# Pooling v for three attention pairs: two additions per pair on VectorE, with a fourth buffer for the pooled loads

## Chip, cores and metric

One Trainium2 chip, one core. The metric is the device time of the kernel in microseconds (us); lower is better. The engines are named as in the profile: PE (TensorE), DVE (VectorE), ACT (ScalarE), POOL (GpSimd), SP (SyncE); PEld is TensorE's loading of weights.

## The reference

Attention on q, k, v of shape 8 x 8 x 576 x 64 (batch, heads, sequence, head width), once on sequences pooled 4:1 by a mean, once in a band of three positions to either side; the two are added, and the sum goes through a gated feed-forward layer (512 to 1536 to 512):

```python
q_d, k_d, v_d = [t.reshape(B, H, Sd, 4, D).mean(axis=3) for t in (q, k, v)]
out_up = np.repeat(sm_attn(q_d, k_d, v_d), 4, axis=2)
mask = np.abs(pos[:, None] - pos[None, :]) < 4
out_local = softmax(where(mask, scale * q @ k.T, -1e9)) @ v
x = (out_up + out_local).transpose(0, 2, 1, 3).reshape(B * S, H * D)
out = (np.maximum(x @ w_gate, 0) * (x @ w_val)) @ w_out
```

## The kernel before

Two heads of one batch entry form a *pair*; there are 32 pairs, numbered `hp` in order of work. Each pair goes through: loads of q, k and v (`emit_in`), the transposed q and k (`emit_qkT`, a transposing DMA from SP's queue for pairs from 9 on), their 4:1 sums (`emit_pool`, L309, one DVE reduction), the scores (`emit_s1_mm`, L389 and L400), the exponentials on ACT (L410, L424), the masking on DVE (`emit_mask`, L416), the products with v (`emit_s2w_mm`, L552 and L560), the division (L570, L575 on ACT, L579 on DVE) and the sum of both attentions into `xT` (`emit_xsum`, L538). After four pairs a 512-token chunk of the feed-forward layer can run: `emit_h_mm` (L622) multiplies by the two weights, L639 (ACT) and L643 (DVE) form the gated product, L652 or, in the later part, the seven products of L719 with sums on DVE (L713) multiply by the last weight.

*Pooled v.* For pairs below 9 it is made by TensorE (`emit_vd`). From pair 9 on, v is loaded a second time by `emit_load_v4` (L297) so that the four positions to be summed lie in one partition (72 partitions of 4 x 256). Two additions follow: `emit_v2` (L355) adds the two halves of each 256, float16 in and float32 out, 512 elements a partition; `emit_v1` (L361) adds the two halves of that, 256 elements a partition, float16 out, into `vd`. Both run on POOL. `v4` is a ring of 3 buffers (`NV4`), `v2` one of 2, `vd` one of 3. `vd` of a pair is read by the matmuls of L560.

*Order.* Every engine's instructions are in an order written out by hand, and each engine takes its own in that order; waits between engines follow from the tiles. The first four pairs are a fill; then come slots `s` = 0 to 7 (`emit_slot`), slot `s` working on pair `hp = s + 4` and loading pair `hp + 4`; then the periods of four pairs (`ORDER`), then a tail. In a slot, `emit_slot_in` comes first. It puts on POOL: the four half loads of q and k of pair `hp + 4`, then the additions of pair `hp + 1` (v2, v1), then the load of v and the v4 load of pair `hp + 4`. So pairs 9, 10 and 11 are pooled in slots 4, 5 and 6; in slot 6 v2 of pair 12 follows at once, and slot 7 does v1 of pair 12 and v2 of pair 13. POOL's queue carries these loads as well as its own arithmetic; SP's carries the transposes and most of the output.

On DVE, slot 5 begins after the weight difference L685 at the end of slot 4, with `emit_pool` of pair 9, then a gate (L643). Slot 6 begins after xsum of pair 9 with the masks of pair 10; slot 7 after xsum of pair 10 with the masks of pair 11. In the periods, `after/3/0` (L1019) is a copy on POOL that makes it wait until the DVE sums of an earlier unit are there and TensorE has read the old ones.

`q32` holds q of the first pair as float32 (L257) until ACT converts it; it isn't used again until the sums of the tail. `zero_sb` feeds warm-up matmuls with zeros.

Of the kernel before, what the change touches and what calls it, by code (L numbers as in the profile page):

```python
# [10 lines left out]
FP16 = mybir.dt.float16  # L11
AF = mybir.ActivationFunctionType
ALU = mybir.AluOpType
# [89 lines left out]
def _dap(t_ap: bass.AP, extra_off: int, dims) -> bass.AP:  # L103
    return bass.AP(tensor=t_ap.tensor, offset=t_ap.offset + extra_off, ap=list(dims))
# [13 lines left out]
def kernel(  # L118
# [10 lines left out]
    nc = tc.nc  # L129
# [13 lines left out]
    LEAD = 4  # L143
    NTP = 9
    NVP = 9
    VS = 7
    NK = NJJ // 2
    B0 = 1
# [4 lines left out]
    keep = ctx.enter_context(tc.tile_pool(name="keep", bufs=1))  # L153
# [2 lines left out]
    ffn = ctx.enter_context(tc.tile_pool(name="ffn", bufs=3))  # L156
    ypool = ctx.enter_context(tc.tile_pool(name="ypool", bufs=4))

    zero_sb = keep.tile([128, 640], FP16, name="zero_sb")
    cst_sb = keep.tile([128, 1368], FP16, name="cst_sb")  # L160
    masks_sb = cst_sb[:, 0:576]
    pool_sb = cst_sb[:, 576:960].rearrange("p (s c) -> p s c", s=3)
# [7 lines left out]
    def ring(n, shape, dtype, name):  # L170
        return [keep.tile(shape, dtype, name=f"{name}{i}") for i in range(n)]

    NL = 7
    NV4 = 3
    PS = 8
    qkfull = ring(NL, [128, 2, 2 * NB * 64], FP16, "qk16_")
    qk16 = [t[0:96] for t in qkfull]
    v4 = ring(NV4, [72, 4, 256], FP16, "v4_")
    v2full = ring(2, [128, 4, 128], FP32, "v2_")
    v2 = [t[0:72] for t in v2full]  # L180
# [6 lines left out]
    vd = ring(3, [72, 2, 192], FP16, "vd_")  # L187
# [6 lines left out]
    q32full = keep.tile([128, 2 * NB * 64], FP32, name="q32")  # L194
# [3 lines left out]
    ps = psum.tile([128, 8, 512], FP32, name="ps")  # L198
# [41 lines left out]
    def head_off(hp):  # L240
        b = (hp // NPB + B0) % B
        return b, (b * H + 2 * (hp % NPB)) * S * D
# [51 lines left out]
    def emit_load_v4(hp):  # L294
        b, off = head_off(hp)
        if hp >= NVP:
            nc.gpsimd.dma_start(  # L297
                v4[hp % NV4], _dap(v, off, [[4 * D, 72], [72 * 4 * D, 4], [1, 4 * D]])
            )

    def emit_qkT(hp):
        nc.sync.dma_start_transpose(
            out=qkT[hp % 4][:, 0 : 2 * S].rearrange("p (n t) -> p n t", t=NQ),
            in_=qk16[hp % NL].rearrange("p i c -> p (i c)"),
        )
# [10 lines left out]
    def emit_qkT_pe(hp, b0, b1, b0_last=False):  # L316
        r, r4, r2 = hp % NL, hp % 4, hp % 2
        sv = qk16[r].rearrange("p i (h j d) -> p i h j d", h=2, d=64)
        blocks = list(range(2 * NB))
        if hp == 0:  # L320
            blocks = blocks[NB:] + blocks[:NB]
        elif b0_last:
            blocks = blocks[4:] + blocks[:4]
        for n in blocks:
            lo = 120 * (n % 4)
            bank = b0 if n < 4 else b1 + n // 4 - 1
            for hh in range(2):
                nc.tensor.matmul(  # L328
                    out=ps[64 * hh : 64 * hh + 64, bank, lo : lo + 120],
                    lhsT=sv[:, n // NB, hh, n % NB, :],  # L330
                    rhs=eyesum_sb,
                    start=True,
                    stop=True,
                )
        big = qkT[r4][:, 0 : 2 * S].rearrange("p (b n t) -> p b n t", b=3, n=4)
        sml = qkd[r2].rearrange("p i t -> p (i t)").rearrange("p (b n t) -> p b n t", b=3, n=4)
        act, dve = nc.scalar.copy, nc.vector.tensor_copy
        if hp == 0:
            plan = ((2, 1, act), (2, 0, act), (1, 1, dve), (1, 0, dve), (0, 1, act), (0, 0, dve))
        elif b0_last:  # L340
            plan = ((1, 1, act), (1, 0, act), (2, 1, dve), (2, 0, dve), (0, 1, dve), (0, 0, act))
        else:
            plan = ((0, 1, act), (0, 0, act), (1, 1, dve), (2, 1, dve), (2, 0, dve), (1, 0, act))
        for i, pooled, copy in plan:
            bank = b0 if i == 0 else b1 + i - 1
            t = ps[:, bank, 0:480].rearrange("p (n t) -> p n t", n=4)
            if pooled:
                copy(out=sml[:, i], in_=t[:, :, 96:120])
            else:
                copy(out=big[:, i], in_=t[:, :, 0:96])  # L350

    def emit_v2(hp):
        if NVP <= hp < NP:
            t, m = v4[hp % NV4], v2[hp % 2]
            nc.gpsimd.tensor_tensor(out=m, in0=t[:, :, 0:128], in1=t[:, :, 128:256], op=ALU.add)  # L355

    def emit_v1(hp):
        if not NVP <= hp < NP:
            return
        m, o = v2[hp % 2], vd[hp % 3]  # L360
        nc.gpsimd.tensor_tensor(  # L361
            out=o.rearrange("p c (x d) -> p x c d", x=3)[:, 0:3:2, :, :],
            in0=m[:, :, 0:64].rearrange("p (h c) d -> p h c d", h=2),
            in1=m[:, :, 64:128].rearrange("p (h c) d -> p h c d", h=2),
            op=ALU.add,
        )
# [64 lines left out]
    def emit_s1(hp, p0):  # L431
        emit_s1_mm(hp, p0)
        for g in range(2):
            emit_exp(hp, p0, g)
            emit_mask(hp, g)
        emit_ed(hp, p0)
# [182 lines left out]
    def emit_h_mm(c, jj, pp, which, kks, out=None):  # L619
        w = (wg_sb, wv_sb)[which]  # L620
        for kk in kks:
            nc.tensor.matmul(  # L622
                out=pair(pp)[:, which, :] if out is None else out,
                lhsT=w[:, kk, bass.ts(jj, 128)],
                rhs=xT[:, kk, c * TCH : (c + 1) * TCH],
                start=(kk == 0),
                stop=(kk == 3),
            )
# [179 lines left out]
    def emit_in(hp, between=lambda: None):  # L808
        if hp >= NP:
            between()  # L810
            return
        if 4 <= hp < NL:
            nc.gpsimd.memset(vw[hp][:, :, 64:128], 1.0)
        emit_load_qk(hp)
        between()
        emit_load_v(hp)
        emit_load_v4(hp)
        if hp in after_load:
            emit_wslice(after_load[hp])
        if hp == 8:  # L820
            for i in range(4):
                emit_wo(i)

    def emit_warm(n):
        for _ in range(n):
            nc.tensor.matmul(
                out=ps[:, 7, :], lhsT=zero_sb[:, 0:128], rhs=zero_sb[:, 128:640], start=True, stop=True
            )

    def emit_fill(hp):  # L830
# [240 lines left out]
    def emit_slot_in(s):  # L1071
        hp = s + LEAD
        if s < VS:
            def pools():
                emit_v2(hp + 1)
                emit_v1(hp + 1)
                if s == VS - 1:
                    emit_v2(hp + 2)
            emit_in(hp + 4, pools)
        else:  # L1080
            emit_v1(hp + 1)
            emit_in(hp + 4, lambda: emit_v2(hp + 2))
        if NTP <= hp + 3 < NP:
            emit_qkT(hp + 3)

    def emit_slot(s, gate):
        c, jj, hp = s // 4, 3 * (s % 4), s + LEAD
        emit_slot_in(s)
        if s == 0:
            emit_qkT_pe(hp, 2, 3)  # L1090
            emit_h_mm(c, jj, 3, 1, range(3))
            emit_h_mm(c, jj, 3, 0, range(1))
            emit_x_pe(hp - 1, 0)
            emit_h(c, jj, 3, ((0, range(1, 4)), (1, range(3, 4))))()
            emit_s1(hp, 2)
            emit_h(c, jj + 1, 0)()
            emit_vd(hp, 6)
            emit_qkT_pe(hp + 1, 2, 3)
            return emit_h(c, jj + 2, 3)
        if s <= 5:  # L1100
            if s == 5:
                emit_pool(hp)
            else:
                gate()
                if s < 4:
                    emit_vd(hp, 1)
            emit_s2t(hp - 1, gate if s == 5 else lambda: None)
            if s == 4:
                emit_wt(0)
        elif gate:  # L1110
            gate()
        if s > 4:
            emit_y(c - 1, s % 4, 1 if s == 5 else 2, 6 if s == 5 else 2, lambda: emit_s1(hp, 4))
            emit_pool(hp + 1)
            if s == PS - 1:
                for step in LEAD_IN.split():
                    kind, arg = step.split("/")
                    emit_step(kind, arg, 1, c)
                return None
            emit_h(c, jj, 0)()  # L1120
            emit_wt(s - 3)
            emit_s2w(hp)
            emit_h(c, jj + 1, 1)()
            emit_h(c, jj + 2, 0)()
            emit_xsum(hp)
            return None
        if s == 4:
            emit_y(c - 1, s % 4, 1)
        else:
            emit_h(c, jj, 0)()  # L1130
        emit_s1(hp, 4)
        if s == 4:
            emit_h(c, jj, 0)()
        emit_h(c, jj + 1, 1)()
        if s == 4:
            emit_wt(1)
            emit_vd(hp, 5)
        else:
            emit_qkT_pe(hp + 1, 4, 0, True)
        return emit_h(c, jj + 2, 3)  # L1140
# [54 lines left out]
```

## Time and profile before

| what | value |
|---|---|
| time, median of 5 runs | 347.5 us (346.84 to 348.41) |
| the profiled execution | 347.17 us, span 345.3 us |
| POOL L355 (v2), 23 times | 1246 ns each |
| POOL L361 (v1), 23 times | 832 ns each |
| POOL L297 (v4 load), 23 times | 739 ns to issue, 6.4 us to landing |
| additions of pair 9 | v2 at 69.04, v1 at 70.28 us |
| additions of pair 10 | v2 at 76.09, v1 at 77.33 us |
| additions of pair 11 | v2 at 82.59, v1 at 83.83 us |

The profile is of one execution. "Busy" is the time in which an engine executed; the bracket behind a timeline line is the time for which its engine stood idle before it, and what it then got. An instruction's duration can hold time in which it is held up by another engine. The share of PE says how little of the span is left for any other engine to show in the time.

### The profile page before, as it was taken

The numbers are of one execution on the slowest core, as the hardware profiler recorded it, in microseconds if no ns is written. First come the engines' busy times: TensorE is split into PE (matmuls) and PEld (weight loads), VectorE is DVE, ScalarE is ACT, GpSimd is POOL, SyncE is SP. The second block draws the span as 40 slices with busy tenths as digits, with TensorE's granted clock in tenths as the row PEclk, the third lists the DMA queues.
The fourth block names the chain that finished last, engine by engine and source line by source line (L and its number), as shares of the span: only waits on it lengthen the run. The fifth ranks groups of instructions, "written<-read, shape, count | busy, mean of one in ns | idle before, by whom it ended". The sixth has DMA issues, their size and how long they took to land.

```text
span 345.3 us, 8168 instructions
## 1 busy us (share of the span) xinstructions
PE 336.4 (97%) x3187; PEld 210.8 (61%) x3187; DVE 294.1 (85%) x529; ACT 215.2 (62%) x410; POOL 189.7 (55%) x238
## 2 busy tenths in 40 slices
PE   6999999999999999999999999999999999999996
PEld 2665555555475656565666656665766557767685
DVE  5895567799899999999999999999999798786892
ACT  3767776677676676677667766776677634344222
POOL 8976556899999993969397797940300000000000
PEclk9999999999999999999999999999999999999999
DMA  9999999999999999999989996992000001001023
GB/s 144 164 171 185 187 189 168 164 171 183 162 153 179 159 180 86 121 148 176 106 102 138 170 124 79 170 125 64 31 32 31 32 0 47 30 33 53 32 69 109
DMA packets 168774, 40.31 MB, mean 117 GB/s; under 512 B 150080, under 2 KB 165664, under 8 KB 168736
## 3 DMA queue, kind: packets, MB, share of 16 engines
q0 software_dynamic: 132960, 22.93, 92.3%
q1 hardware_dynamic: 35056, 15.79, 24.5%
q10 hardware_dynamic: 720, 1.08, 0.9%
q8 instruction: 25, 0.41, 0.6%
q14 instruction: 13, 0.11, 0.1%
HBM read 46.45 MB, written 9.44 MB: 162 GB/s over the span
## 4 chain that ended last, share of the span: by engine, by line
PE 83%; DVE 10%; ACT 2%; DMA 2%; issue 2%; ACTq 0%; POOLq 0%
PE ps L622 44%; PE ps L719 18%; PE ps L929 4%; PE ps L552 3%; PE ps L652 2%; PE ps L389 2%; PE ps L328 2%; PE ps L400 2%; DVE xn L579 2%; DVE gT L643 2%; DVE ee L416 2%; DMA qk<-in_k_dram 2%; PE ps L560 1%; DVE xo L713 1%; ACT rden L570 1%
## 5 line engine op out<-in xcount | busy, mean ns | idle before, releaser
L622 PE MATMUL ps<-xT,wv_sb 128*128 128x512 f16 x432 | 109.3, 379 | 0.0
L622 PE MATMUL ps<-xT,wg_sb 128*128 128x512 f16 x352 | 89.1, 380 | 0.1
L643 DVE TENSOR_TENSOR gT<-r,ps 128x512 f16<-128x512 f16 x88 | 59.1, 680 | 11.9 <-ACT r L639 6.3
L639 ACT ACTIVATE r<-ps 128x512 f16<-128x512 f32 x88 | 52.3, 594 | 26.9 <-PE ps L622 26.7
L622 PEld LDWEIGHTS <-wv_sb 128*128 128x128 f16 x432 | 41.0, 98 | 41.7 <-issue 0.2
L622 PEld LDWEIGHTS <-wg_sb 128*128 128x128 f16 x352 | 32.0, 98 | 32.3 <-DVE xT L615 0.6
L579 DVE TENSOR_TENSOR xn<-ps,rden 64x720 f16<-64x720 f32 x46 | 41.6, 905 | 4.2 <-ACT rden L575 2.9
L570 ACT ACTIVATE rden<-ps 64x720 f32<-64x720 f32 x46 | 35.2, 765 | 15.7 <-PE ps L560 14.7
L410 ACT ACTIVATE ee<-ps 112x576 f16<-112x576 f32 x64 | 38.1, 647 | 10.8 <-PE ps L400 9.8
L267 POOL DMA_DIRECT2D qk<-in_q_dram x46 | 33.9, 742 | 6.7 <-DMA wo_sb<-in_moe_w_out_dram 2.8
L267 POOL DMA_DIRECT2D qk<-in_k_dram x46 | 33.8, 740 | 3.8 <-DMA v<-in_v_dram 2.8
L416 DVE TENSOR_TENSOR ee<-ee,cst_sb 112x576 f16<-112x576 f16 x64 | 33.0, 539 | 2.8 <-ACT ee L410 2.2
L292 POOL DMA_DIRECT2D vw<-in_v_dram x30 | 28.7, 958 | 8.8 <-PE ps L560 2.9
L719 PEld LDWEIGHTS <-gT 128*128 128x128 f16 x288 | 28.2, 98 | 8.6
L309 DVE TENSOR_REDUCE qkd<-qkT 128x288 f16<-128x1152 f16 x23 | 30.9, 1343 | 0.3 <-DMA qkT<-qk 0.3
L355 POOL TENSOR_TENSOR v<-v 72x512 f32<-72x512 f16 x23 | 28.7, 1246 | 1.9 <-DMA v<-in_v_dram 1.4
L719 PEld LDWEIGHTS <-xo 128*128 128x128 f16 x240 | 22.7, 97 | 6.1 <-DVE xo L713 0.3
L753 ACT COPY q<-ps 128x256 f32<-128x256 f32 x39 | 14.5, 371 | 18.5 <-PE ps L719 18.2
L719 PE MATMUL ps<-wo_sb,gT 128*128 128x256 f16 x192 | 24.9, 273 | 0.0
L538 DVE TENSOR_TENSOR xT<-xn 128x576 f16<-128x576 f16 x28 | 24.0, 857 | 0.6
L939 ACT COPY vw<-ps 128x256 f32<-128x256 f32 x30 | 10.8, 373 | 20.7 <-PE ps L929 13.8
L552 PE MATMUL ps<-ee,vw 112*128 112x96 f16 x276 | 20.5, 205 | 1.0 <-DVE ee L416 1.0
(116 smaller groups left out, 571.4 us busy)
## 6 DMA issues: line engine op xcount, KB each, us to landing
out_dram<-y_sb SPq DMA_DIRECT2D x20, 256.0 KB, 3.6
vw<-in_v_dram POOLq DMA_DIRECT2D x30, 168.0 KB, 6.3
qk<-in_q_dram POOLq DMA_DIRECT2D x46, 72.0 KB, 6.0
qk<-in_k_dram POOLq DMA_DIRECT2D x46, 72.0 KB, 6.1
v<-in_v_dram POOLq DMA_DIRECT2D x23, 144.0 KB, 6.4
out_dram<-y_sb SPq DMA_DIRECT2D x22, 128.0 KB, 1.7
wg_sb<-in_moe_w_gate_dram POOLq DMA_DIRECT2D x4, 384.0 KB, 10.0
wv_sb<-in_moe_w_val_dram POOLq DMA_DIRECT2D x4, 384.0 KB, 10.8
```

The source lines that it names most:

```text
L267: nc.gpsimd.dma_start(dst.rearrange("p (j h d) -> p j h d", h=2, d=64)[:, :, hh, :], _dap(src, off + hh * S * D, [[D, 96], [NQ * D, NB], [ ...
L292: nc.gpsimd.dma_start(t, _dap(v, base, [[D, WK], [NQ * D, n], [1, D]]))
L309: nc.vector.tensor_reduce(out=qkd[hp % 2].rearrange("p i t -> p (i t)"), in_=qkT[hp % 4][:, 0 : 2 * S].rearrange("p (t f) -> p t f", f=4), ...
L410: nc.scalar.activation(out=o, in_=ps[0:WK, p0 + 2 * g : p0 + 2 * g + 2, 0:288], func=AF.Exp, scale=scale)
L416: nc.vector.tensor_tensor(out=o, in0=o, in1=_sap(masks_sb, (0, WK), 288 * g, [[0, 2], [1, 288]]), op=ALU.mult,)
L552: nc.tensor.matmul(out=ps[:, bank, NQ * j : NQ * j + NQ], lhsT=vflat[:, v0 : v0 + 128], rhs=e[:, hh, lo : lo + NQ], start=True, stop=True,)
L570: nc.scalar.activation(out=rden[lo : lo + 64], in_=ps[de : de + 64, 4 + 2 * hh : 6 + 2 * hh, 0:360], func=AF.Ln)
L579: nc.vector.tensor_tensor(out=xn[lo : lo + 64], in0=ps[lo : lo + 64, 4 + 2 * hh : 6 + 2 * hh, 0:360], in1=rden[lo : lo + 64], op=ALU.mult,)
L622: nc.tensor.matmul(out=pair(pp)[:, which, :] if out is None else out, lhsT=w[:, kk, bass.ts(jj, 128)], rhs=xT[:, kk, c * TCH : (c + 1) * TCH],
L639: nc.scalar.activation(out=r1, in_=pair(pp)[:, 0, :] if h1 is None else h1, func=AF.Relu)
L643: nc.vector.tensor_tensor(out=gT[c % 2][:, jj, :], in0=r1, in1=pair(pp)[:, 1, :] if h2 is None else h2, op=ALU.mult)
L719: nc.tensor.matmul(out=out, lhsT=left[:, i, :], rhs=right[i], start=(first and i == 0), stop=(i == NK - 1), skip_group_check=True,)
```

## The change

For pairs below `VVP` = 12, that is 9 to 11, both additions are issued on DVE, and at the head of the slot of the pair itself (5 to 7) rather than on POOL one slot earlier. The float32 result of v2 goes to `q32`'s memory. `v4` gets a fourth buffer, and `zero_sb` loses 128 columns: the warm-up matmuls read the same zeros for both operands. Pairs from 12 on stay on POOL in their old places.

```diff
+    VVP = 12
-    zero_sb = keep.tile([128, 640], FP16, name="zero_sb")
+    zero_sb = keep.tile([128, 512], FP16, name="zero_sb")
-    NV4 = 3
+    NV4 = 4
...
+    def pooling(hp):
+
+        if hp < VVP:
+            return nc.vector, q32full[0:72, 0:512].rearrange("p (a b) -> p a b", a=4)
+        return nc.gpsimd, v2[hp % 2]
+
     def emit_v2(hp):
         if NVP <= hp < NP:
-            t, m = v4[hp % NV4], v2[hp % 2]
-            nc.gpsimd.tensor_tensor(out=m, in0=t[:, :, 0:128], in1=t[:, :, 128:256], op=ALU.add)
+            t, (eng, m) = v4[hp % NV4], pooling(hp)
+            eng.tensor_tensor(out=m, in0=t[:, :, 0:128], in1=t[:, :, 128:256], op=ALU.add)
 
     def emit_v1(hp):
         if not NVP <= hp < NP:
             return
-        m, o = v2[hp % 2], vd[hp % 3]
-        nc.gpsimd.tensor_tensor(
+        (eng, m), o = pooling(hp), vd[hp % 3]
+        eng.tensor_tensor(
...
-                out=ps[:, 7, :], lhsT=zero_sb[:, 0:128], rhs=zero_sb[:, 128:640], start=True, stop=True
+                out=ps[:, 7, :], lhsT=zero_sb[:, 0:128], rhs=zero_sb, start=True, stop=True
...
             def pools():
-                emit_v2(hp + 1)
-                emit_v1(hp + 1)
                 if s == VS - 1:
                     emit_v2(hp + 2)
             emit_in(hp + 4, pools)
...
         c, jj, hp = s // 4, 3 * (s % 4), s + LEAD
+        if hp < VVP:
+            emit_v2(hp)
+            emit_v1(hp)
         emit_slot_in(s)
```

## The prediction

> **What bounds the kernel now.** I read the page first (busy shares, then the chain that ended last), then TensorE's timeline between 55 and 132 us for the places where it stands still, then VectorE's and GpSimd's timelines of the same stretch, because the change moves work between these two.
>
> ```profile
> PE 336.4 (97%) x3187; PEld 210.8 (61%) x3187; DVE 294.1 (85%) x529; ACT 215.2 (62%) x410; POOL 189.7 (55%) x238
> PE 83%; DVE 10%; ACT 2%; DMA 2%; issue 2%; ACTq 0%; POOLq 0%
> ```
>
> TensorE is busy for 336.4 of 345.3 us, so anything done on another engine counts only where TensorE waits for it. The slots concerned are 5 (TensorE from 66.68 us), 6 (76.88) and 7 (86.04 to 95.82); their TensorE timeline has one wait, and the next one comes in the first period of the steady loop:
>
> ```profile
> 90.92 0.29 PE L552 MATMUL ps<-ee,vw 112*128 112x96 f16 x3 [0.46 <-DVE ee L416]
> 115.22 0.25 PE L389 MATMUL ps<-qkd 64*72 64x144 f16 x2 [0.33 <-DVE xn L579]
> ```
>
> Measured from start to start the first costs 0.62 us (the pair of L560 before it starts at 90.23 and needs 0.07) and the second 0.50 us (L719 starts at 114.07 and needs 0.65). Together 1.12 us: the most that the change can win near its place. The stages, with columns length, then PE, PEld, DVE, ACT, POOL busy:
>
> ```profile
> 82.00:90.00 8.00, 8.00 (x68) 4.06 (x65) 7.63 (x9) 5.70 (x9) 7.89 (x9) 1.00 1.79 156
> 90.00:97.00 7.00, 6.54 (x64) 3.71 (x61) 6.00 (x8) 4.36 (x9) 6.99 (x9) 1.00 2.11 179
> 97.00:105.00 8.00, 8.00 (x79) 5.83 (x72) 7.87 (x14) 6.04 (x12) 7.98 (x11) 1.00 2.12 156
> 105.00:115.00 10.00, 9.89 (x85) 5.74 (x83) 9.92 (x14) 6.67 (x12) 9.61 (x14) 1.00 1.80 188
> ```
>
> VectorE has 1.0 us idle in 90 to 97, and only 0.2 from 97 to 115: there a delay of VectorE is passed on. GpSimd is full all through. Then VectorE's and GpSimd's lines that decide:
>
> ```profile
> 65.39 0.95 DVE L685 TENSOR_TENSOR wt<-wo_sb,xT 128x1536 f16<-128x1536 f16 x1
> 66.26 1.34 DVE L309 TENSOR_REDUCE qkd<-qkT 128x288 f16<-128x1152 f16 x1
> 68.58 0.69 DVE L643 TENSOR_TENSOR gT<-r,ps 128x512 f16<-128x512 f16 x1 [0.98 <-ACT r L639]
> ...
> 82.59 1.16 POOL L355 TENSOR_TENSOR v<-v 72x512 f32<-72x512 f16 x1
> 82.67 1.90 DVE L685 TENSOR_TENSOR wt<-wo_sb,wt 128x1536 f16<-128x1536 f16 x1
> ...
> 87.94 1.27 POOL L361 TENSOR_TENSOR vd<-v 72x256 f16<-72x256 f32 x1
> 88.56 2.31 DVE L416 TENSOR_TENSOR ee<-ee,cst_sb 112x576 f16<-112x576 f16 x2
> 89.46 1.40 DVE L416 TENSOR_TENSOR ee<-ee,cst_sb 112x576 f16<-112x576 f16 x1
> ...
> 137.11 0.19 POOL L1019 COPY seen<-xo 128x1 f16<-128x1 f16 x1 [5.69 <-PE ps L719]
> ```
>
> The L685 beside a GpSimd addition takes 1.90 us, the one at 65.39 takes 0.95. The two masks of pair 11 take 2.31 us where those of pair 10 (79.39) take 0.82: this is what TensorE waits for at 90.92. And at 137.11 GpSimd has waited 5.69 us for TensorE, so a head start of GpSimd ends there.
>
> **What the Trainium skill says.** "SBUF — State Buffer", section "Who interferes with whom": a VectorE instruction with both inputs in SBUF and a GpSimd instruction that reads SBUF exclude each other, the later one waits for the whole of the earlier. The trace agrees: L685 at 82.67 has its own 0.95 us left from the end of L355 (83.75), and L361 behind it (83.83) takes 1.33 instead of 0.72. The section also says that `tensor_tensor` does not hold up descriptor generation. The trace is not so clean: the mask at 89.46 takes 0.95 us more than its usual 0.45 while GpSimd only issues DMAs. "VectorE: DVE Perf Modes", section "The perf-mode tier table": `tensor_tensor` gains its double rate only for 16-bit tensors; v2 writes float32, v1 reads it, so both go at the single rate. The same page, section on the errata, prices such an addition at (N+151)/0.96 ns: 691 ns for 512 elements, 424 for 256. The trace agrees for L538 (576 elements: 757 by the formula, 0.75 to 0.76 us shown).
>
> **The change part by part.** *Removed from GpSimd*: v2 and v1 of pairs 9, 10, 11: 1.16+1.28, 1.17+0.72, 1.16+1.33 = 6.8 us in slots 4, 5, 6. TensorE waits for no GpSimd work there, so this is worth nothing by itself. Everything queued behind goes earlier: per slot four qk loads, the v load, the v4 load, later v1(12), v2(13). Adding up GpSimd's own durations it reaches the v4 load of pair 15 at about 87 us instead of 94.16. The new wait is here: that load's buffer (15 mod 4) is pair 11's, which VectorE reads at about 88.6 to 89.3; behind it stand the loads of pairs 16 and 17; the first is needed for the transpose issued with scores(13), near 106, so nobody waits for them. The DMA queue may not take the issues that fast (GpSimd waited for it at 66.27 and 67.50), which only shrinks the head start. At L1019, about 105, it now has to wait for the sums of L713 that end at 102.05: some 3 us of lead are left, and none at 137.
>
> *Added to VectorE*: per slot v2 then v1, at the head of slots 5, 6, 7. v1 reads v2's output, so it starts after v2's end: 0.69+0.03+0.36 (v1's 0.42 less the 0.06 by which starts overlap in this trace) = 1.08 us from v2's start to the next instruction. Three times 1.08 = 3.2 us. Not in the trace of before: bounds are 0.42+0.28 if the double rate held (L904 and L713 of 512 and 256 elements) and 1.08+0.95 if one is held up as the mask at 89.46 was; I take 1.08.
>
> *Slot 5*: after L685. L309 goes from 66.26 to 67.34 and ends at 68.68; TensorE starts scores(9) at 68.97. The gate (L643) sat idle for 0.98 and goes from 68.58 to 68.62. Hidden, with 0.29 us to spare; past that scores(9) are late. The masks at 70.89, which lost 0.5 to v1(9) on GpSimd, get it back; no one waited.
>
> *Slot 6*: after xsum (L538, 78.72). The masks of pair 10 end at 81.3 instead of 80.2; TensorE needs the second at 82.0. If v2(12), now about 78.2 on GpSimd, holds xsum up by 0.6, they end at 81.9: just in time. Behind: L685 keeps its 0.95, so it ends near where it did (84.57), before L579 at 84.81. Hidden.
>
> *Slot 7*: L579 at 84.81 waits for ScalarE's inv as before, so the chain to xsum (87.89) stands. v2(11) starts at 88.56, v1 ends at 89.70, the masks run 89.64 to 90.46 if GpSimd holds nothing: v1(12), which cost them time at 87.94, has gone to about 81, and GpSimd waits for v2(11). TensorE goes on at 90.51 instead of 90.92: **0.4 us won**. L309(12) starts at 90.4 instead of 90.78; no lag is carried past the 0.5 and 0.4 us idle at 92.64 and 93.73.
>
> *First period*: GpSimd's additions meet other VectorE instructions. Before, four of these lost 0.42 (L713 at 99.35), 0.53 (100.97), 0.60 (L538, 106.35) and 0.84 us (L713, 111.91). About as many will meet; zero, with a bound of the 0.50 at 115.22 won to one v2 (1.16) lost.
>
> *Fourth v4 buffer*: v4 loads waited 0.3 us four times for v2 on GpSimd; off the path. *zero_sb by 128 columns*: about 0.13 us less memset; the first real matmul waits for k to land (6.56). Zero.
>
> Sum: -0.4 us. The profiled execution took 347.17, so 346.8; the median of the runs shown is 0.33 above it, so **347.1**.
>
> **Rivals.** A, *both waits go*: slot 7 is clean and the period's collisions thin out, -1.1 us: 346.4. For it: 2.4 us of VectorE's time there was lost to collisions. Against: GpSimd has the same six additions to do in that stage, only 3 us earlier.
> B, *the slot 7 masks end later than before* (the other side): four two-input instructions stand where two stood, GpSimd issues v4(15) and qk loads beside them, and two are held up by 0.95 as at 89.46. Masks end at 92.36, TensorE goes on 1.5 us later: 349.0. It decides once hold-ups in slot 7 exceed 0.41 us (2.31 less 1.08 less 0.82). For: the full VectorE behind. Against: the mask at 79.76, beside the same kind of issue, took 0.45.
> C, *the lag shows elsewhere*: the additions of slot 5 outlast 0.29 us, or one more collision in 97 to 115: +0.6: 348.1. For: no idle time there. Against: slot 5 has no GpSimd addition beside it now.
>
> **How the numbers follow.** Forecast 0.50, A 0.18, B 0.20, C 0.12. Its own range, with 0.5 us either way for the period and the spread between executions, is 346.3 to 347.9. With B's and most of A's and C's inside, 8 in 10 is 345.9 to 349.1. A measurement here can tell about 0.3%, 1.04 us. Faster: 0.11 of A, 0.07 of the forecast = 0.18. Slower: 0.15 of B, 0.05 of C, 0.05 of the forecast = 0.25. Within: 0.57.
>
> **What would show it.** v2 and v1 on VectorE near 0.69 and 0.42 us; scores(9) at 68.97 without a wait; L685 in slot 6 back to 0.95; the masks of pair 11 ending near 90.46, the L552 wait there under 0.2; v4(15) issued right after v2(11); GpSimd waiting at L1019 and again near 137. Wrong, if VectorE's additions take over 1.3 us a pair, if TensorE waits in slots 5 or 6, or if the steady loop past 137 runs otherwise than before.

## The result and the profile after

The changed kernel is slower by about 1 us: median 348.83 us of 43 executions (345.70 to 353.22) against 347.67 us of 80 of the kernel before on the same chips, a ratio of 1.0029 [1.0016, 1.0041] (the bracket is the 95% interval; the ratio leaves out the executions that ran in a slower state of the chip). The time lies inside the range of the forecast (345.9 to 349.1), but the forecast was 0.4 us faster, and the move is the other way, at the size that was called the least that can be told from no change. The profiled execution took 348.34 us, its span is 346.4 us: 1.17 us over the profiled execution of before. In the changed kernel's listing the line numbers are 7 or 8 higher: v2 is L362, v1 L368, the masks L423, the weight difference L692, the products with v L559.

The page of the changed kernel first, its busy line and the engines' shares of the chain that ended last:

```profile
PE 337.5 (97%) x3187; PEld 210.7 (61%) x3187; DVE 295.1 (85%) x535; ACT 215.1 (62%) x410; POOL 183.1 (53%) x232
...
PE 87%; DVE 6%; ACT 2%; DMA 2%; issue 1%; DVEq 0%; ACTq 0%; POOLq 0%
...
vw<-in_v_dram POOLq DMA_DIRECT2D x30, 168.0 KB, 7.2
qk<-in_q_dram POOLq DMA_DIRECT2D x46, 72.0 KB, 6.7
```

The change did what it says: six instructions moved from POOL to DVE, POOL is 6.6 us less busy, DVE 1.0 us more. (The six additions take 3.3 us there; other instructions of DVE are shorter by the rest.) The last two lines tell of the loads: a plain load of v now takes 7.2 us from issue to landing, a half load of q 6.7 us. The page of before has for the same:

```profile
vw<-in_v_dram POOLq DMA_DIRECT2D x30, 168.0 KB, 6.3
qk<-in_q_dram POOLq DMA_DIRECT2D x46, 72.0 KB, 6.0
```

VectorE's timeline of the changed kernel, slots 5 to 7 (start, duration, then engine, line and operation):

```profile
66.21 0.68 DVE L362 TENSOR_TENSOR q<-v 72x512 f32<-72x512 f16 x1
66.92 0.42 DVE L368 TENSOR_TENSOR vd<-q 72x256 f16<-72x256 f32 x1
67.27 1.34 DVE L310 TENSOR_REDUCE qkd<-qkT 128x288 f16<-128x1152 f16 x1
...
80.64 0.82 DVE L423 TENSOR_TENSOR ee<-ee,cst_sb 112x576 f16<-112x576 f16 x2
...
83.23 2.08 DVE L692 TENSOR_TENSOR wt<-wo_sb,wt 128x1536 f16<-128x1536 f16 x1
...
88.97 0.68 DVE L362 TENSOR_TENSOR q<-v 72x512 f32<-72x512 f16 x1
89.69 0.42 DVE L368 TENSOR_TENSOR vd<-q 72x256 f16<-72x256 f32 x1
90.03 0.82 DVE L423 TENSOR_TENSOR ee<-ee,cst_sb 112x576 f16<-112x576 f16 x2
```

The reader sees the price of the additions (from 66.21 to 67.27, 1.06 us a pair), masks of pair 10 that end at 81.46 us, in time, and L692 in slot 6 that is still held up: 2.08 us where 0.95 was forecast. What holds it is in GpSimd's timeline of the same kernel; the bracket gives the idle time before the instruction and what released it:

```profile
71.70 0.73 POOL L268 DMA_DIRECT2D qk<-in_q_dram  x1 [2.17 <-DMA vw<-in_v_dram]
73.81 0.73 POOL L268 DMA_DIRECT2D qk<-in_q_dram  x1 [1.37 <-DMA v<-in_v_dram]
...
79.66 0.73 POOL L268 DMA_DIRECT2D qk<-in_q_dram  x1 [1.44 <-DMA vw<-in_v_dram]
81.08 0.72 POOL L268 DMA_DIRECT2D qk<-in_q_dram  x1 [0.69 <-DMA v<-in_v_dram]
81.79 1.44 POOL L268 DMA_DIRECT2D qk<-in_k_dram  x2
83.32 1.17 POOL L362 TENSOR_TENSOR v<-v 72x512 f32<-72x512 f16 x1
```

The addition at 83.32 is v2 of pair 12. It was forecast near 78.2, because all six removed additions stood ahead of it. In the kernel before:

```profile
85.13 1.15 POOL L355 TENSOR_TENSOR v<-v 72x512 f32<-72x512 f16 x1
```

In place of the additions, GpSimd now stands before the next half load of q until an earlier load of its own queue has landed. The stretch 64 to 104 us of both kernels (length, then PE, PEld, DVE, ACT, POOL busy with counts, clock, DMA share, GB/s), before first:

```profile
64.00:104.00 40.00, 39.54 (x352) 22.18 (x350) 36.17 (x48) 27.20 (x45) 38.45 (x47) 1.00 1.94 168
```

```profile
64.00:104.00 40.00, 39.96 (x352) 22.32 (x351) 36.52 (x55) 27.23 (x46) 28.90 (x38) 1.00 2.02 156
```

POOL falls from 38.45 to 28.90 us busy, with nine instructions fewer, and its loads run at 156 GB/s instead of 168. The freed time became waiting: the brackets with a DMA as releaser add up to 1.16 us in this stretch before and to 10.12 us after.

TensorE's timeline of the changed kernel shows where this profile's time went:

```profile
86.70 0.25 PE L396 MATMUL ps<-qkd 64*72 64x144 f16 x2
...
87.12 0.25 PE L396 MATMUL ps<-qkd 64*72 64x144 f16 x2
...
90.63 0.29 PE L559 MATMUL ps<-ee,vw 112*128 112x96 f16 x3
...
110.67 0.29 PE L559 MATMUL ps<-ee,vw 112*128 112x96 f16 x3 [1.02 <-DVE ee L423]
```

From the scores of pair 11 (86.70) to those of pair 12 (96.55) it needs 9.85 us; before it was 10.01. Then 1.02 us are lost at 110.67, on the masks of pair 13, which stand at 107.30 (1.17 us long) and 108.99 (1.63 us). The first runs beside GpSimd's v2 of pair 15 (105.98 to 108.15), the second beside its v2 of pair 14 (109.16 to 110.30). In this pair of profiles, then, slot 7 gained 0.2 us, and the first period lost 0.7 us: scores of pair 12 to those of pair 14 took 19.39 us where they took 18.65. That was the first theory. It fell, as the next section tells.

### The profile page after: what moved, and what is told of

It is laid out like the page before. It is cut to its first block, busy times and chain, and to the rows that moved or that the text cites. A ratio compares the mean times of both kernels' runs of the same rounds, so it can differ in the third digit from the quotient of the medians.

```text
span 346.4 us, 8175 instructions
## 1 busy us (share of the span) xinstructions
PE 337.5 (97%) x3187; PEld 210.7 (61%) x3187; DVE 295.1 (85%) x535; ACT 215.1 (62%) x410; POOL 183.1 (53%) x232
## 3 DMA queue, kind: packets, MB, share of 16 engines
q10 hardware_dynamic: 720, 1.08, 1.0%
## 4 chain that ended last, share of the span: by engine, by line
PE 87%; DVE 6%; ACT 2%; DMA 2%; issue 1%; DVEq 0%; ACTq 0%; POOLq 0%
PE ps L629 46%; PE ps L726 19%; PE ps L936 4%; PE ps L559 3%; PE ps L659 3%; PE ps L396 2%; PE ps L407 2%; PE ps L329 2%; DVE ee L423 2%; PE ps L567 2%; DMA qk<-in_k_dram 1%; DVE xn L586 1%; DVE gT L650 1%; ACT ee L417 1%; DVE xo L481 1%
## 5 line engine op out<-in xcount | busy, mean ns | idle before, releaser
L586 DVE TENSOR_TENSOR xn<-ps,rden 64x720 f16<-64x720 f32 x46 | 41.6, 905 | 4.5 <-ACT rden L582 3.3
L423 DVE TENSOR_TENSOR ee<-ee,cst_sb 112x576 f16<-112x576 f16 x64 | 33.6, 546 | 3.1 <-ACT ee L417 2.3
L362 POOL TENSOR_TENSOR v<-v 72x512 f32<-72x512 f16 x20 | 26.1, 1304 | 1.0 <-DMA v<-in_v_dram 0.5
L545 DVE TENSOR_TENSOR xT<-xn 128x576 f16<-128x576 f16 x28 | 22.9, 817 | 0.6
L559 PE MATMUL ps<-ee,vw 112*128 112x96 f16 x276 | 20.6, 205 | 1.6 <-DVE ee L423 1.6
```

The source lines that it names most:

```text
L423: nc.vector.tensor_tensor(out=o, in0=o, in1=_sap(masks_sb, (0, WK), 288 * g, [[0, 2], [1, 288]]), op=ALU.mult,)
L559: nc.tensor.matmul(out=ps[:, bank, NQ * j : NQ * j + NQ], lhsT=vflat[:, v0 : v0 + 128], rhs=e[:, hh, lo : lo + NQ], start=True, stop=True,)
L586: nc.vector.tensor_tensor(out=xn[lo : lo + 64], in0=ps[lo : lo + 64, 4 + 2 * hh : 6 + 2 * hh, 0:360], in1=rden[lo : lo + 64], op=ALU.mult,)
```

## The experiments

Two kinds of number are used: the ratio to the kernel before, with its 95% interval; and, because single profiles differ by more than the effect, three distances read from the starts of the scores in each profile. The table is referred to below (us; "11 to 12" is slot 7; "DMA waits" are GpSimd's brackets with a DMA as releaser between 64 and 104 us; v2(12) is the start of that addition on GpSimd, counted from the start of the scores of pair 8, since the executions don't start alike):

```
kernel             11 to 12  12 to 14  14 to 31  DMA waits  v2(12)
before               10.01     18.65    151.43      1.16    24.58
before2               9.85     19.66    152.69      2.34    24.28
zero512               9.70     19.28    150.94      1.01    24.28
warm_b                9.39     19.13    151.40      2.33    22.64
addr_b                9.39     19.58    151.60      0.99    23.63
changed (after)       9.85     19.39    151.78     10.12    22.82
again                 9.69     19.38    151.38      8.36    23.87
a_delay              10.29     18.97    151.73      8.00    23.98
after3               10.65     18.81    152.34      7.65    24.02
```

The first five have before's order of work in these stages, the last four have the change's.

**The change once more, and the first period.** Is the 1.02 us wait at 110.67 the cost? *again* is the changed kernel unaltered. *shift* moves, in the first period, v2 of pair 15, the copy of L1026, v1 of pair 15 and v2 of pair 14 on GpSimd behind the loads that followed, so that the first of them no longer meets the masks of pair 13:

```diff
+            moved = ["v2/b/0", "after/3/0", "v1/a/1", "v2/a/0"]
+            toks = [t for t in toks if t not in moved]
+            i = toks.index("v4/a/1")
+            toks[i:i] = moved
```

> The changed kernel once more, for a second profile. All theories: ratio to the kernel before about 1.003 (1.0015 to 1.0045). What the profile is to tell: theory DMA (the loads are limited by the DMA queue, GpSimd gains no head start, and its additions of pairs 14 and 15 land on the masks of pair 13) expects GpSimd idle for 5 us or more between 66 and 100 us, waiting for DMAs, and a TensorE wait of 0.5 to 1.5 us at the second L559 group near 110.7. Theory VectorE (the 3.2 us of additions are passed on) expects the lost time inside slots 5 to 7 or as a lag of VectorE from 92 us on.

> The changed kernel with one difference: in the first period GpSimd does v2(15), the copy of L1019, v1(15) and v2(14) after the loads of q, k of pair 18 and v of pair 17, some 3 to 4 us later, so that they miss the masks of pair 13 (107 to 110.6). Theory DMA with the collision: the two masks take 0.45 us each, the wait of 1.0 us at 110.67 is gone, ratio 0.999 to 1.001. Theory VectorE: as the changed kernel, 1.003.

*again*: 1.0029 [1.0009, 1.0049], the same loss. *shift* did what it was to do, and lost: 1.0064 [1.0038, 1.0091]. The masks of pair 13 went back to 0.46 and 0.45 us, the scores of pairs 12 to 14 came in 18.2 us, as short as in any profile; but what was moved is late elsewhere. Its timeline of TensorE:

```profile
118.15 0.29 PE L559 MATMUL ps<-ee,vw 112*128 112x96 f16 x3 [0.85 <-DVE ee L423]
...
137.75 0.83 PE L726 MATMUL ps<-wt,xo 128*128 128x256 f16 x6 [1.37 <-DVE xo L720]
```

The additions that the first period holds cost something there, too. *before2*, the kernel before unaltered, asks whether that cost is the change's:

> The kernel before once more, for a second profile of it. All theories: ratio 1.000 (0.998 to 1.002). Theory phase (what decides is where GpSimd's additions fall against VectorE's two-input instructions on the path) expects TensorE to lose about 0.6 us in slot 7 and less than 0.6 us between the scores of pairs 13 and 14 again.

It gave 0.9998 [0.9979, 1.0017], and its profile lost time at the very same place: 19.66 us from the scores of pair 12 to 14, more than any profile of the changed kernel. Over the table the mean of that column is 19.26 us with before's order and 19.14 us with the change's. The collision comes with the execution, with and without the change; with only one profile of each kernel it looked like the whole explanation.

**Without the colliding additions.** *b_no* and *a_no* leave out the pooling additions of pairs 13 to 16, on the kernel before and on the changed one (the pooled v of these pairs is left out; the rest is computed):

```diff
-        if NVP <= hp < NP:
+        if NVP <= hp < NP and hp not in range(13, 17):
```

> The kernel before without the pooling additions of pairs 13 to 16 (left out: their pooled v, so the results of these pairs differ). It clears the stretch 97 to 130 us of GpSimd's arithmetic. Theory phase: no loss between the scores of pairs 12 and 14 (18.2 to 18.5 us for the two), 0.4 to 1.0 us faster than before: 0.997 to 0.999.

> The changed kernel without the pooling additions of pairs 13 to 16 (left out as in b_no). Against b_no it tells what the change costs when GpSimd's additions cannot meet VectorE in 97 to 130 us. Theory phase: no slower than b_no, by slot 7's gain some 0.2 to 0.5 us faster: 0.996 to 0.999 of before. Theory VectorE and theory buffer: the full 0.7 to 1.0 us slower than b_no.

*b_no* 0.9983 [0.9961, 1.0004], *a_no* 1.0004 [0.9977, 1.0030]. Between the two lie 0.0021, some 0.7 us (the standard error of that difference is about 0.4): that points to a cost which stays when the collisions are gone, but at under two standard errors it does not show it. *b_no* also gives the floor of slot 7, since TensorE stands still nowhere in it: 9.38 us from the scores of pair 11 to 12.

**The same additions drawn forward.** *early* (on the changed kernel) and *early_b* (on the kernel before) put v1 of pair 13 and v2 and v1 of pair 14 on GpSimd at the end of slot 7, where the head start was to have left room:

```diff
+            toks.remove("v1/a/0>")
+            i = next(i for i, t in enumerate(toks) if t == "qk/a0/0>")
+            toks[i:i] = ["v1/a/0>", "v2/a/0>", "v1/b/0>"]
+        elif n == 0:
+            toks.remove("v2/a/0")
+            toks.remove("v1/b/0")
```

> The changed kernel, with v1(13), v2(14) and v1(14) of GpSimd drawn forward to the end of slot 7 (near 94 us, where VectorE works on PSUM), so that only v2(15) and v1(15) stand near the masks of pair 13. Theory phase: the 1.0 us wait near 110.7 is gone or under 0.3 us, ratio to before 0.998 to 1.001, some 1 us under the changed kernel. Theory VectorE: as the changed kernel, 1.003.

> The kernel before with the same three additions drawn forward. Theory phase: the wait in slot 7 stays (0.6 us or more, as v1(12) still meets the masks), what was lost near 115 (0.5 us) shrinks; 0.998 to 1.001. Against early it tells what moving pairs 9 to 11 is worth once the collision is out of the way: phase expects early to be 0.3 to 0.6 us faster than this, VectorE expects it to be 1 us slower.

*early* 1.0014 [0.9986, 1.0042], *early_b* 0.9988 [0.9968, 1.0007]: neither can be told from the kernel before, and *early_b*, the lowest of the versions that compute everything but for one below, is no proven gain.

**The work on GpSimd put back or taken away.** *noadd* is the changed kernel without the additions of pairs 9 to 11 on either engine (pooled v of these pairs is left out). *filler* is the changed kernel in which GpSimd does them too, in their old places, into memory that nobody reads then:

```diff
-        if NVP <= hp < NP:
+        if VVP <= hp < NP:
```

```diff
+                fill_v(hp + 1)
```

> The changed kernel without the six additions of pairs 9 to 11 (left out: pooled v of these pairs, whose products then use old contents). VectorE is 3.2 us lighter, GpSimd as in the changed kernel. Theory DMA: still slower than before, 1.001 to 1.004, within 0.1% of the changed kernel, with a wait of TensorE for the masks of pair 13 near 110. Theory VectorE: 1.000 or below, 1 us or more under the changed kernel.

> The changed kernel, and besides GpSimd does the six additions of pairs 9 to 11 at their old places too, with results that nobody reads. VectorE carries 3.2 us more than before, GpSimd is as busy as before. Theory phase: GpSimd's order of events is that of before, so the 0.8 us lost between the scores of pairs 13 and 14 is not lost (under 0.4 us), while slot 7 loses 0.5 to 1.5 us as VectorE is held up there; ratio to before 1.000 to 1.003. Theory VectorE (its added time is what costs): slower than the changed kernel, 1.004 or more.

*noadd*: 1.0011 [0.9981, 1.0041]. Even with nothing on VectorE and nothing on GpSimd there is no gain that can be seen, and GpSimd's DMA waits stay at 7.75 us. That is the plainest sign that the six additions on GpSimd were covered. *filler*: 1.0037 [1.0005, 1.0070], not better than the change itself; its profile lost 1.0 us from the scores of pair 8 to those of pair 12. Of that, 0.8 us lie ahead of the scores of pair 9, which waited because v1 of pair 9 took 1.26 us on VectorE (from 66.69) instead of 0.42 while GpSimd issued loads (66.08 to 67.53). It doesn't separate the theories.

**Where on VectorE.** *dve3* puts the additions on VectorE one slot earlier (slots 4 to 6), with three buffers and the old `zero_sb`. *slack* puts those of pair 10 ahead of `emit_pool(10)` in slot 5 and those of pair 11 behind `emit_pool(11)` in slot 6, that is off the masks of slot 7. *vvp11* gives pair 11 back to GpSimd, in slot 6, and keeps 9 and 10 on VectorE:

```diff
-        if hp < VVP:
-            emit_v2(hp)
-            emit_v1(hp)
+        if hp + 1 < VVP:
+            emit_v2(hp + 1)
+            emit_v1(hp + 1)
```

```diff
-        if hp < VVP:
+        if hp == NVP:
...
+            if s == 5:
+                emit_v2(hp + 1)
+                emit_v1(hp + 1)
...
+            if s == 6:
+                emit_v2(hp + 1)
+                emit_v1(hp + 1)
```

```diff
-    VVP = 12
+    VVP = 11
...
+                if hp + 1 >= VVP:
+                    emit_v2(hp + 1)
+                    emit_v1(hp + 1)
```

> The six additions of pairs 9 to 11 on VectorE, but in slots 4 to 6 as before, with three v4 buffers and the old zero_sb. Tells engine from buffer. Theory buffer (the fourth buffer and the shifted addresses cost about 0.2%): 0.999 to 1.001. Theory phase (GpSimd without these additions runs into the DMA queue and falls behind by 100 us): as the changed kernel, 1.002 to 1.004, GpSimd waiting 4 us or more for DMAs in 66 to 103 us, v2(15) starting less than 1.2 us before the scores of pair 13. Theory VectorE: 1.002 to 1.004 with TensorE late inside slots 4 to 6.

> The changed kernel with two of VectorE's three pairs of additions moved to where VectorE stood idle: pair 10's into slot 5 ahead of the pooling reduction of pair 10 (it waited 1.46 us there for the transpose), pair 11's into slot 6 behind that of pair 11. Slot 7 then begins with the masks. Theory slot 7 (1.08 us of additions ahead of the masks of pair 11, and every hold-up beside them, go to TensorE): scores of pair 11 to scores of pair 12 in 9.4 to 9.6 us instead of 9.7 to 10.65, the first of these masks under 2.4 us behind the scores of pair 11; ratio 1.000 to 1.0015. If the cost lies behind slot 7 alone: 1.003 as before, slot 7 no shorter. GpSimd waits 6 us or more for DMAs in 64 to 104 us in either case.

> The changed kernel with only pairs 9 and 10 on VectorE; pair 11's additions stay on GpSimd in slot 6, four buffers. Theory slot 7: 9.4 to 10.0 us between the scores of pairs 11 and 12, ratio 1.000 to 1.002. If the cost lies in pairs 9 and 10 or behind slot 7: 1.002 to 1.003. GpSimd's waits for DMAs in 64 to 104 us: about 2 us less than with all three moved, 5 to 7 us.

*dve3*: 1.0049 [1.0032, 1.0067]. One slot earlier the load of pair 9 hasn't landed, as VectorE's timeline of it shows:

```profile
59.86 0.69 DVE L362 TENSOR_TENSOR q<-v 72x512 f32<-72x512 f16 x1 [2.57 <-DMA v<-in_v_dram]
```

That is not all: in slot 6 xsum took 2.10 us (usually 0.75) at 80.27 with v2 of pair 12 beside it on GpSimd, and from the scores of pair 8 to those of pair 11 it is 26.80 us instead of 26.0. Slot 7, where the masks then come first, took 9.39 us, the floor.

*slack*: 1.0030 [1.0012, 1.0049], nothing won. The masks of pair 11 lost nothing (90.82, 0.82 us for both), but in slot 6 VectorE is now behind. Its timelines, VectorE's first and TensorE's after it:

```profile
80.59 2.15 DVE L423 TENSOR_TENSOR ee<-ee,cst_sb 112x576 f16<-112x576 f16 x2
```

```profile
88.97 0.25 PE L396 MATMUL ps<-qkd 64*72 64x144 f16 x2 [0.56 <-DVE xn L586]
```

The masks of pair 10 met v2 of pair 12 on GpSimd (2.15 us for two that take 0.82), the additions of pair 11 behind them were held up as well (0.90 and 0.83 us, at 83.93 and 84.87), the division `xn` came late, and the scores of pair 11 waited for it: 10.14 us from the scores of pair 11 to 12. *vvp11*: 1.0010 [0.9990, 1.0030], slot 7 in 9.39 us, the floor, and DMA waits of 4.36 us. With the 1.06 us of pair 11 gone from in front of its masks most of the loss seems to go, though the interval overlaps with that of the change.

**The buffers and the zeros.** *buf4* is the kernel before with the fourth `v4` buffer and the smaller `zero_sb`, *zero512* with the smaller `zero_sb` alone, *warm_b* with the old `zero_sb` of which only 512 columns are zeroed and read (so no other tile moves), *addr_b* is *zero512* with `ones_sb` filled ahead of `zero_sb`, so that the warm-up starts as late as before, and *a_delay* is the changed kernel with that same order:

```diff
-    NV4 = 3
+    NV4 = 4
...
-    zero_sb = keep.tile([128, 640], FP16, name="zero_sb")
+    zero_sb = keep.tile([128, 512], FP16, name="zero_sb")
```

```diff
-    nc.vector.memset(zero_sb, 0.0)
+    nc.vector.memset(zero_sb[:, 0:512], 0.0)
```

> The kernel before with only the fourth v4 buffer and the smaller zero_sb; the additions stay on GpSimd in slots 4 to 6. Theory DMA and theory VectorE: 1.000 (0.999 to 1.001). Theory buffer (the addresses or the ring cause it): 1.003.

> The kernel before with only zero_sb cut to 512 columns, so that every later buffer lies 256 bytes lower. Theory buffer in its form addresses: 1.002. All others: 1.000 (0.998 to 1.002).

> The kernel before with all buffers where they were, but zero_sb zeroed and read in 512 columns only: TensorE's warm-up starts 0.06 us earlier. If the warm-up's timing is what zero512 paid for (TensorE at half rate in some executions at 6 to 12 us): 1.0015, as zero512. If addresses or chance: 1.000 (0.998 to 1.002).

> The kernel before with zero_sb of 512 columns (later buffers 256 bytes lower) and ones_sb zeroed first, so that the warm-up starts as late as before. If addresses are what zero512 paid for: 1.0015. If the warm-up's timing or chance: 1.000.

> The changed kernel with the same swap, so that the warm-up starts as late as in the kernel before. If the warm-up's timing is a part of the change's cost: 1.001 to 1.0015. If the cost is all in slots 5 to 7 and after: 1.0025 to 1.003.

*buf4* 1.0019 [1.0001, 1.0036], *zero512* 1.0009 [0.9989, 1.0028], *warm_b* 1.0003 [0.9984, 1.0023], *addr_b* 0.9984 [0.9959, 1.0009], *a_delay* 1.0049 [1.0030, 1.0068]. *buf4* alone looked like a cost of its own, and led to the other four. An earlier warm-up (*warm_b*) costs nothing that can be seen, moved tiles (*addr_b*) neither, and putting the start-up of the changed kernel back (*a_delay*) mends nothing. What the fourth buffer alone costs was not tried without the smaller `zero_sb`; *buf4* puts both together at 0.66 us, with an interval from 0.03 to 1.25 us. (Two of the expectations speak of 1.0015 for *zero512*; its ratio on record is 1.0009.)

**The change a third time.** *after3* was run for a further profile of slot 7:

> The changed kernel on the same chip as the three others, and a third profile of it: 1.003 (1.001 to 1.0045). In its profile the load queue theory expects GpSimd to wait 5 us or more for DMAs between 66 and 103 us once more, and the masks of pair 13 to be held up by 1 us or more in all.

1.0014 [0.9988, 1.0040], and the clearest view of the mechanism. Its timelines of slot 7, VectorE, GpSimd, TensorE:

```profile
88.45 1.63 DVE L362 TENSOR_TENSOR q<-v 72x512 f32<-72x512 f16 x1
90.12 0.42 DVE L368 TENSOR_TENSOR vd<-q 72x256 f16<-72x256 f32 x1
90.46 0.82 DVE L423 TENSOR_TENSOR ee<-ee,cst_sb 112x576 f16<-112x576 f16 x2
```

```profile
87.16 0.74 POOL L368 TENSOR_TENSOR vd<-v 72x256 f16<-72x256 f32 x1
87.84 1.48 POOL L268 DMA_DIRECT2D qk<-in_q_dram  x2
89.31 1.44 POOL L268 DMA_DIRECT2D qk<-in_k_dram  x2
90.77 1.52 POOL L362 TENSOR_TENSOR v<-v 72x512 f32<-72x512 f16 x1
```

```profile
91.05 0.29 PE L559 MATMUL ps<-ee,vw 112*128 112x96 f16 x3 [1.02 <-DVE ee L423]
```

v2 of pair 11 takes 1.63 us instead of 0.68, that is 0.95 us more, while GpSimd does no arithmetic and only issues loads; the masks start at 90.46 instead of 89.5; TensorE waits 1.02 us for them. In *a_delay* the same wait is 0.30 us. In *after* and *again* there is no bracket, and time is lost in small pieces: in *after*, 0.21 us between the two halves of the scores of pair 11 (87.12 is where the second division, L586, ends, late in the wake of L692), 0.16 us ahead of the first masked product (90.63) and 0.08 ahead of the second, 0.45 of the 0.47 us over the floor.

Measured from start to start against *b_no*, the masked products of pair 11 come late in every profile that has pair 11's additions at the head of slot 7: by 0.2 to 1.3 us in the four of the table, *shift*, *a_no*, *early* and *filler*. In the four runs without these additions there (*noadd*, *dve3*, *slack*, *vvp11*) they are not late at all; with before's order they are late by 0 to 0.6 us. What holds the masks back differs from one execution to the next. In *again* it is little more than the additions themselves, 0.31 us. In *a_delay* it is also GpSimd's arithmetic: L692 takes 1.88 us beside v2 of pair 12, xsum 1.05 us at 88.32 beside v1 of pair 12. In *after3* it is the issuing of loads. In *early* v2 of pair 11 takes 1.64 us from 89.63, beside GpSimd's v2 of pair 13 (89.49 to 90.72).

Put together, slot 7 over the profiles with pair 11's additions at its head and no longer on GpSimd (the four of the table, *shift* 9.76, *a_no* 9.58, *early* 10.53) has a mean of 10.05 us; over all with before's order there (the five of the table, *b_no* 9.38, *early_b* 10.00, *buf4* 9.49) 9.65 us: +0.40 us, with a standard error of 0.19.

## Why the prediction was right and wrong

**The price of the additions: right.** 0.68 and 0.42 us against 0.69 and 0.42, 1.06 against 1.08 us a pair. (The memset of `zero_sb` got 0.06 us shorter, 0.33 to 0.27 us, where about 0.13 was put; it was taken at zero either way.)

**Slots 5 and 6 hidden: right.** The scores of pair 9 start at 68.92 (forecast 68.97), without a wait; the masks of pair 10 end at 81.46 (81.3 to 81.9). From the scores of pair 8 to those of pair 11 it is 26.0 us before and in *again*, *after3* and *a_delay*, 26.2 in *after*.

**The removed work: this is the step that failed.** The forecast said "Everything queued behind goes earlier" and placed v2 of pair 12 near 78.2, v1 of pair 12 at about 81 and the v4 load of pair 15 near 87. Measured in *after*: v2 of pair 12 at 83.32, v1 of it at 86.61, the v4 load at 93.43 (94.16 before). Over the table v2 of pair 12 starts 23.7 us behind the scores of pair 8 on the mean with the change and 23.9 us without it: of 6.8 us of freed time 0.2 us arrived. The rest shows in the column of the DMA waits (8.5 us on the mean against 1.6). The step had a caution beside it, that the queue might not take the loads that fast, but it was put down as something that "only shrinks the head start"; in fact it took nearly all of it, and slot 7 was worked out as if it hadn't. The page of before could have told: its line of the DMA engines' busy share (tenths, 40 slices of the span) stands at nine through the whole first half:

```profile
DMA  9999999999999999999989996992000001001023
```

Slots 4 to 7, 60 to 97 us, lie in the eighth to twelfth slice, and in the changed kernel's page the line reads nine there again, at fewer bytes. Loads that went to DMA engines as busy as this brought GpSimd no head start here when they were issued sooner. (The waits are measured; that the full DMA engines are their cause is argued, as no run made these less busy.)

**L692 back to 0.95 us: half right.** 2.08 us in *after* and 1.88 in *a_delay*, beside v2 of pair 12; 0.95 in *again* and *after3*, where that addition came behind it. (In the kernel before it is 0.82 us of L685 that follow the end of GpSimd's addition, 83.75 to 84.57, not its whole 0.95 as the forecast read it.) By the forecast it should have come long before it in all of them.

**Slot 7: wrong sign.** -0.4 us was forecast, +0.40 ± 0.19 us is the mean. The forecast took the clean case: nothing of GpSimd's beside four two-input instructions, because v1(12) "has gone to about 81". In *b_no* the first masked product of pair 11 starts 3.54 us behind the start of its scores. With before's order the first mask starts 2.0 to 2.8 us behind the scores, with the change 3.2 to 4.1, and it takes 0.45 us itself: the additions use up what the masks had to spare, and every hold-up comes on top. Before, a hold-up of 0.82 us (xsum in *addr_b*) was absorbed whole, and of 0.95 us on the first mask TensorE lost 0.46 in *before2* and 0.31 in *zero512*; in *after3* all of it reaches TensorE. The head start that didn't come is behind a part of this only: in *after* and *a_delay* VectorE is held up by additions of pair 12 that were to be long done, in *again* and *after3* by no more than 0.12 us of xsum. And there was less to win than was thought: the 0.62 us wait of the profiled execution of before was taken as the standing cost of slot 7, but with that order the mean over eight profiles is only 0.27 us above the floor of 9.38. The forecast's own slot 7, 10.01 less 0.41 us, is 9.60 us, against that mean of 9.65: even the clean case had next to nothing to win.

**Rival B named the mechanism and oversized it.** Its place (the masks of pair 11), its price (0.95 us for a two-input instruction beside issued loads) and its point of decision (hold-ups over 0.41 us) are what *after3* shows; in *a_delay* the hold-ups came from arithmetic instead. It counted two beside issued loads in every execution; of four profiles, TensorE waits for the masks 1.02 us in one, 0.30 in another, and less than a bracket shows in two. *vvp11*, which takes only pair 11 away, and *noadd*, which takes all three, both go most of the way back to the kernel before, as this asks, though their intervals overlap with the change's. *slack*, which moved the additions out of slot 7, should have gone back too and didn't: the places tried in slots 5 and 6 were not free either.

**Rival A fell, and so did the places that C named:** slot 7 isn't clean, the period's collisions did not thin out on the mean nor grow, and slot 5 had no wait. That a lag shows elsewhere, as C also said, is not excluded.

**The first period at zero: right as a mean**, 19.26 us against 19.14, though any two profiles differ by up to 1 us. "GpSimd waiting at L1019" did not come: in all four profiles with the change the copy runs without a wait (at 108.11 in *after*). The second wait, near 138, did come, 3.35 to 6.39 us long in these four and 5.33 to 5.69 in the five with before's order.

**What stays open.** Of +1.0 us, 0.4 us is found in slot 7. The nine profiled spans of the table differ by no more than that on the mean (346.1 us with before's order, 346.5 with the change), so these profiles may not hold all of the cost. The column 14 to 31 is 151.61 us on the mean of before's order and 151.81 with the change, which the scatter of single profiles doesn't separate; the start, up to the scores of pair 8, is 60.85 and 60.70 us.

One place further on stands out. From the scores of pair 26 to those of pair 27 every profile with before's order takes 8.33 us; *after*, *again* and *a_delay* take 8.67, 8.61 and 8.71 (*after3* 8.33). One of the two masks of pair 26 takes 1.26 to 1.37 us there instead of 0.46, beside a v2 on GpSimd that had waited for its load. *noadd* has it too (8.81), so VectorE's additions are not needed for it. It was picked out afterwards from some thirty such distances, and no run tested it.

The fourth buffer with the smaller `zero_sb` stays a rival for a part: the interval of *buf4* (1.0019) overlaps with the change's. Against it stand *noadd*, *early* and *vvp11*, which have both and ratios of 1.0010 to 1.0014, with intervals that reach up to 1.0042.

## What to carry to other kernels

Work taken off an engine that also issues the loads need not give it a head start: here 0.2 of 6.8 us arrived, and GpSimd waited at its loads instead. Look at the busy share of the DMA engines and at the time to landing before any later instruction is dated forward. VectorE, 85% busy here, had its slack in particular places: 1.06 us put in front of the masks that TensorE needs turned hold-ups that had been absorbed, in whole or in part, into waits. Where the effect is under 1 us, take several profiles of the kernel before as the base: the 0.62 us wait of the first one was in none of the four others of the table at that size.

## What the runs showed of the hardware

- A VectorE instruction with both inputs in SBUF was held up while GpSimd only issued DMAs: 0.68 to 1.63 us in *after3*; in *early*, xsum took 1.53 us (usually 0.75) at 107.96 beside the issues at 107.64 and 108.58. The Trainium skill, "SBUF — State Buffer", section "Who interferes with whom", says that `tensor_tensor` did not stall DMA, and infers that the two need different interfaces. The traces show the other direction, an addition held up, though not what it is in the issuing that holds it; and not beside every issue (0.68 us for the same addition in *shift*, beside issues at 87.85).
- The mutual exclusion with GpSimd's arithmetic that this section describes is confirmed: L692 took 2.08 us from 83.23, and 0.82 us of that lie behind the end of v2 of pair 12 at 84.49. It was the earlier of the two in the trace, by 0.09 us, and waited none the less.
- Loads that are issued sooner may land later: in *after*, those of v issued between 64 and 80 us took 11.0 us on the median where they took 6.6, at 151 GB/s instead of 172. Over the table the medians are 9.7 to 11.0 us with the change, 6.6 to 7.6 with before's order.
- TensorE's first microseconds vary: in *again* three warm-up matmuls at 7.75 took 1.29 us where before's at 7.31 took 0.82, and the scores of pair 1 came 0.87 us later than in before. Of the kernels with before's order, *zero512*, *warm_b* and *buf4* showed the like. The scores of pair 1 came later than 13 us in 8 of the 13 profiles in which the warm-up starts earlier than before, and in 1 of the 7 others; the times of *warm_b* and *a_delay* do not show a cost of it.
